# A decode kernel of attention beside a Mish layer: an early end of the Tile context, a PSUM bank of its own for w1, and w2 behind the turn

## The chip, the cores and the metric

The kernel runs on one core of a Trainium2 chip. Its time is the device time in microseconds. Three runs gave 1307.58, 1308.07 and 1309.73 us; the median, 1308.07, is the time before. The engines are called PE (TensorE), DVE (VectorE), ACT (ScalarE), POOL (GpSimd) and SP (SyncE, which here only issues transfers). PEld is the loading of weights into PE.

## The reference

One token for each of 8 batches (D = 512) goes through a layer norm, and the normed row feeds two branches whose results are added to x:

```
xn = layernorm(x)
A  = softmax(q k^T / sqrt(128)) v  @ wo      # q = xn @ wq, 32 query heads, 8 K/V heads,
                                             # 8192 cached positions, heads of 128
Bm = mish(xn @ w1 + b1) @ w2                 # F = 1792; mish(h) = h * tanh(softplus(h))
out = x + A + Bm
```

All is float32. The caches of K and V are 268 MB each, so 561 MB are read once and nearly nothing is written.

## The kernel before, in words

The work is cut into 16 packs p; each has two batches b and a pair of K/V heads. A K block or a V block of one (p, b) is 8.4 MB. Three places in SBUF take what is loaded: `kva` and `kvb`, for K, V, w1 and w2, and `kvw`, for a quarter of wq or wo. `plan` puts each load on a list in a fixed order (K(p, b), then V(p-1, b)), and `pump` issues the head of the list on SP as soon as the place it wants is free; `release` frees a place when the last product that read it is done. SP's queue is in order, so a load whose place is held also holds those behind it.

What the places see: wq, then w1 (into `kva`) and K(0,0) (into `kvb`) at the start; K(0,1) goes into `kva` behind w1; from then on K goes into `kvb` (which has some room for the next K's overlap) and V into `kva`. At the end V(15,0) goes into `kvb`, V(15,1) into `kva` in two parts, and behind V(15,0) come, in turn, w2's first part, half of wo's last quarter, w2's second part, the other half of wo, and w2's last part.

The start, pack "before" (enter(0)): `setup` clears some buffers on DVE, norms x and builds selectors; `queries` forms the queries of four heads in the PSUM bank H on PE, which DVE scales and turns and `expand`s into qT; `mish` forms xn @ w1 + b1, also in H, so its first product waits until DVE has read the queries there; DVE tells SP (a `relay`, a wait that passes a signal on) that w1 is read, and copies the result out.

In a pack: `scores` (64 products into c), `rows` (into s), `maximum` (DVE and PE), `expand` for the next pack's queries, `exponents` (ACT and DVE), `weights`, and `values` for the pack before (into o), then `gather` and `merge`. PE, DVE and ACT run these as loops over the packs 1 to 15.

The end (enter(PACKS)): the last `values`, `gather(1)`, then the products of aT with w2 (`down`), `merge(1)`, `collect(1)`, `turn` (which brings the heads' results into oW, copied out by DVE and ACT), `last_outputs` (oW with wo) and more `down`, all summed up in H; DVE copies H to acc, SP sends it out. `unread` is filler: products that nobody reads.

The class Program records each operation with its waits; `emit` then issues them, within `tc.tile_critical`; `tc.close` ends the Tile context, with two barriers of all engines, and `finish` clears the semaphores and waits for the transfer out. As all operations are issued from one helper, all have line 390 in the profile; they are told apart by their tiles (c<-kvb,qT are scores, o<-kva,pt values, h<-kvb,aT the products of w2, h<-kvw,oW those of wo, h<-acc,gsel the bias of w1).

Of the kernel before, what the change touches and what calls it, by code (L numbers as in the profile page):

```python
# [28 lines left out]
FG = F // G  # L29
# [4 lines left out]
PB = 2  # L34
# [75 lines left out]
class Program:  # L110
# [8 lines left out]
    def __init__(self, nc):  # L119
        self.nc = nc  # L120
        self.ops, self.count = [], {}
        self.know = {e: {} for e in ENGINES}
        self.seen = {}
        self.on_chip, self.psum = set(), set()
        self.pack, self.name, self.zone, self.at = None, None, "before", 0
        self.sends, self.numbers = {}, {}
        self.starts, self.sems = {}, {}

# [56 lines left out]
    def add(self, op, after=()):  # L185
# [161 lines left out]

    def finish(self, stream):

        (last,) = (c for c in self.signals if c[0] == stream)  # L350
        numbers = sorted(s.num for c, s in self.sems.items() if c != last)
        assert numbers == list(range(numbers[0], numbers[-1] + 1))
        self.nc.gpsimd.sem_clear(range(numbers[0], numbers[-1] + 1))
        self.nc.sync.wait_ge(self.sems[last], 16).then_inc(self.sems[last], -16)

    def emit(self):
        self.schedule()
        self.verify()
        nc, sems, unit = self.nc, self.sems, {}
        for c, given in sorted(self.signals.items(), key=lambda x: x[0][0] == "out"):  # L360
            sems[c] = nc.alloc_semaphore("_".join(x for x in c if x))
            unit[c] = given[0].unit

        def lower(engine, c, n):
            n *= unit[c]
            if n:
                getattr(nc, engine).wait_ge(sems[c], n).then_inc(sems[c], -n)

        def values(o):
            if o.place[1] == "loop" and o.engine in LOOPED:  # L370
                return [(c, n * unit[c]) for c, n in self.body[o.place].items()]
            top = {}
            for g in o.waits:
                c = self.channel(g)
                n = self.number[g]
                if o.engine in LOOPED and o.place[1] == "after":
                    n -= self.lowered(c, END, self.final)
                top[c] = max(n * unit[c], top.get(c, 0))
            return list(top.items())

        def issue(o, pack):
            engine = getattr(nc, o.engine)
            *first, last = values(o) or [None]
            for c, n in first:
                engine.wait_ge(sems[c], n)
            if o.method in ("settle", "relay"):
                got = engine.wait_ge(sems[last[0]], last[1])
            else:
                args, kw = (o.make(pack), {}) if o.make else (o.args, o.kw)
                got = getattr(engine, o.method)(*args, **kw)  # L390
                if last:
                    got.wait_op(sems[last[0]], last[1], "sem-ge")
            if c := self.channel(o):
                got.then_inc(sems[c], o.unit)

        for o in self.ops:
            if o.place[1] == "before" or o.engine not in LOOPED:
                issue(o, o.pack)
        for engine, parts in self.bodies():
# [19 lines left out]
            for o in self.ops:  # L419
                if o.place[1] == "after" and o.engine == engine:  # L420
                    issue(o, o.pack)


@with_exitstack
def kernel(
# [173 lines left out]
    def setup():  # L599
# [78 lines left out]
    def setup_w1(xs):  # L678
# [13 lines left out]

        pool.memset(pt, 0.0, after=[read])

# [30 lines left out]

    def expand(later):

        for b in range(PB):
            dve.vary(
# [9 lines left out]

    def scores(b, k, order, relay=False):  # L740
# [11 lines left out]
        read = prog.relay("scalar", "sync", last) if relay else None  # L752
        act.copy(sc, C[b])
        return read
# [11 lines left out]

    def maximum():
# [179 lines left out]
    def mish(w1_sb):  # L947


        hp = H[:, :FG]  # L950
        for g in range(G):
# [73 lines left out]
    for p in range(PACKS):  # L1025
        prog.enter(p)
        for b in range(PB):
            k = landed.pop(("k", p, b))
            n = PB * p + b - (p > 0)
            order = range(KR) if n % 2 == 0 else range(KR - 1, -1, -1)  # L1030
            read = scores(b, k, order, relay=(p, b) == (0, 1))
            release(("k", p, b), read)
# [10 lines left out]
            elif p > 0:  # L1043
                merge(0)
            rows(b)
            if b == 1:
                maximum()
                expand(1)
                exponents(0)
                fold()  # L1050
# [52 lines left out]
    tc.compile()  # L1103
    prog.finish("out")

# [37 lines left out]
```

## Time and profile before

| | |
|---|---|
| median of three runs | 1308.07 us |
| profiled execution | 1307.95 us |
| its span, first to last instruction | 1305.8 us |
| PE busy | 875.6 us, 67% of the span |
| DVE busy | 389.9 us, 30% |
| ACT busy | 122.2 us, 9% |
| POOL busy | 4.8 us |
| read from HBM | 561.01 MB |
| mean granted clock of PE | 0.834 |

All rows of the trace come from the one profiled execution; times in them are microseconds from the start of its span. In a stretch's row stand its bounds and length, then for PE, PEld, DVE, ACT and POOL the busy time and the number of instructions, then the granted share of PE's clock, the mean busy share of the 16 DMA engines (which can be over 1 in a short stretch) and GB/s. In the chain, each row has a start, a duration and what the time went to; "DMA" is the time from a transfer's issue to its landing. In the timeline a row has start, duration, engine, line, operation, out<-in, the shape and how many instructions were merged; in brackets the engine's idle time before it and what ended it. A float32 product of PE shows as two records.

### The profile page before, as it was taken

How to read it: one execution, taken by the hardware profiler on the slowest of the kernel's cores; microseconds unless marked ns; L12 is line 12 of the kernel's file. 1: busy time of each engine (PE TensorE's matmuls, PEld its weight loads, DVE VectorE, ACT ScalarE, POOL GpSimd, SP SyncE). 2: the span in 40 equal slices, each digit the busy share in tenths (PEclk: the TensorE clock that was granted, in tenths of full speed). 3: DMA queues.
4: the chain of work that ended last, by engine and by line, in shares of the span. 5: the costliest groups of instructions: out<-in, count | busy, mean ns of one | idle time of the engine just before them, and what ended most of it. 6: DMA issues, size and time to landing. Idle time of an engine off the chain costs nothing.

```text
span 1305.8 us, 11349 instructions
## 1 busy us (share of the span) xinstructions
PE 875.6 (67%) x4798; PEld 274.0 (21%) x4798; DVE 389.9 (30%) x596; ACT 122.2 (9%) x294; POOL 4.8 (0%) x10
## 2 busy tenths in 40 slices
PE   4886657766657765687666686665875755766568
PEld 1221112212112211122111222111221211222113
DVE  5350504305051230521405132052320515014061
ACT  0020202001020110201102020010200102001020
POOL 1000000000000000000000000000000000000000
PEclk8887788887789877898887888778887779878878
DMA  9999999999999999999999999999999999999997
GB/s 402 446 422 442 422 444 424 442 426 442 426 442 426 440 424 444 424 442 426 442 426 442 417 448 428 440 426 434 434 434 434 434 434 428 440 428 440 428 434 324
DMA packets 11409, 561.21 MB, mean 430 GB/s; under 512 B 1276, under 2 KB 1408, under 8 KB 1544
## 3 DMA queue, kind: packets, MB, share of 16 engines
q1 hardware_dynamic: 11376, 561.06, 99.5%
q8 instruction: 7, 0.11, 0.0%
q10 hardware_dynamic: 24, 0.02, 0.0%
q14 instruction: 2, 0.02, 0.0%
HBM read 561.01 MB, written 0.07 MB: 430 GB/s over the span
## 4 chain that ended last, share of the span: by engine, by line
DMA 63%; PE 34%; DVE 2%; issue 0%; POOL 0%; ACT 0%; DVEq 0%; ACTq 0%; SPq 0%
DMA kvb<-in_kT 60%; PE c L390 30%; PE h L390 2%; DMA kva<-in_kT 2%; PE o L390 1%; DMA kvb<-in_w 1%; DVE raw L390 1%; PE m L390 0%; DVE pt L390 0%; DVE wide L390 0%; DVE nm L390 0%; DVE st L390 0%; PE s L390 0%; POOL pt L390 0%; DMA sc<-in_x 0%
## 5 line engine op out<-in xcount | busy, mean ns | idle before, releaser
L390 PE MATMUL c<-kvb,qT 128*64 128x512 f32 x1984 | 497.7, 665 | 327.3 <-DMA kvb<-in_kT 325.6
L390 PEld LDWEIGHTS c<-kvb,qT 128*64 128x64 f32 x1984 | 153.3, 154 | 671.7 <-DMA kvb<-in_kT 354.5
L390 PE MATMUL o<-kva,pt 128*32 128x512 f32 x1984 | 241.5, 643 | 25.4 <-DMA kva<-in_v 24.9
L390 DVE TENSOR_REDUCE nm<-s 128x1 f32<-128x1024 f32 x16 | 19.6, 1225 | 444.6 <-PE s L390 444.6
L390 DVE STREAM_TRANSPOSE raw<-wide 128x2048 f32<-128x2048 f32 x36 | 125.4, 3483 | 15.9 <-ACT wide L390 14.0
L390 ACT COPY sc<-c 128x512 f32<-128x512 f32 x32 | 18.8, 586 | 974.7 <-PE c L390 974.7
L390 PEld LDWEIGHTS o<-kva,pt 128*32 128x32 f32 x1984 | 65.4, 117 | 192.8 <-issue 149.2
L390 ACT ACTIVATE wide<-s,nms 128x512 f32<-128x512 f32 x128 | 88.0, 688 | 129.8 <-DVE nms L390 66.3
L390 DVE TENSOR_TENSOR oT<-m,rt 128x16 f32 (+1 forms) x17 | 3.0, 175 | 230.9 <-PE m L390 230.9
L390 DVE TENSOR_SCALAR os<-o,isel 128x128 f32<-128x128 f32 x32 | 11.2, 350 | 153.9 <-PE o L390 153.9
L390 DVE TENSOR_TENSOR pt<-raw 64x256 f32<-64x256 f32 x128 | 53.5, 418 | 1.9
L390 PE MATMUL s<-sc,csel 64*128 64x512 f32 x128 | 37.1, 657 | 8.7 <-ACT sc L390 7.1
L390 DVE TENSOR_TENSOR qT<-qc,bsel 128x1024 f32<-128x1024 f32 x34 | 40.1, 1222 | 1.0
L390 DVE TENSOR_TENSOR raw<-raw 128x1024 f32<-128x1024 f32 x32 | 39.2, 1225 | 2.9
L390 DVE SCALAR_TENSOR_TENSOR os<-o,isel,os 128x128 f32<-128x128 f32 x96 | 33.7, 351 | 3.4
L390 ACT ACTIVATION_READ_ACCUMULATOR wide<-s,nms 128x1 f32 x128 | 24.7, 193 | 0.0
L390 PE MATMUL m<-hsel,os 128*128 128x8 f32 x66 | 12.7, 265 | 10.5 <-DVE lsel L390 10.5
L390 PE MATMUL m<-ident,nm 128*1 128x128 f32 x16 | 4.4, 276 | 21.6 <-DVE nm L390 21.6
L390 PE MATMUL h<-kvw,xnT 128*64 128x512 f32 x64 | 16.9, 676 | 0.0
L390 DVE TENSOR_SCALAR wide<-h 128x512 f32<-128x512 f32 x16 | 11.1, 691 | 19.2 <-PE h L390 18.8
L390 PEld LDWEIGHTS m<-hsel,os 128*128 128x128 f32 x66 | 10.1, 193 | 24.7 <-issue 12.4
L390 PE MATMUL c<-kva,qT 128*64 128x512 f32 x64 | 14.0, 594 | 0.6 <-DMA kva<-in_kT 0.6
(91 smaller groups left out, 169.4 us busy)
## 6 DMA issues: line engine op xcount, KB each, us to landing
kvw<-in_wq SPq DMA_DIRECT2D x4, 2048.0 KB, 30.1
kvw<-in_wo SPq DMA_DIRECT2D x3, 2048.0 KB, 30.7
kva<-in_v SPq DMA_DIRECT2D x1, 6144.0 KB, 24.6
kva<-in_w SPq DMA_DIRECT2D x1, 3584.0 KB, 15.9
kva<-in_v SPq DMA_DIRECT2D x1, 2048.0 KB, 29.1
kvb<-in_w SPq DMA_DIRECT2D x1, 2048.0 KB, 14.1
kvw<-in_wo SPq DMA_DIRECT2D x2, 1024.0 KB, 18.1
kvb<-in_w SPq DMA_DIRECT2D x1, 1024.0 KB, 17.9
```

Of the source, the lines that this page charges most:

```text
L390: got = getattr(engine, o.method)(*args, **kw)
```

## The change

It has five parts.

- The program is prepared first (`prepare`: schedule, verify, semaphores). Within the Tile context only the first operations are issued: of each engine those ahead of its first operation that waits (`emit_first`). These are the two transfers of ACT, SP's first three, six clearings on DVE and one on POOL. Then the context is closed, with its barriers, and the rest is issued outside it. At the end SP passes the wait of its transfer out on to POOL (semaphore `end`), which clears the semaphores while SP waits for the landing.
- xn @ w1 + b1 goes into the bank O[1] instead of H; DVE clears that bank at the start. POOL, and not DVE, relays to SP and to DVE that the products are done.
- V(0,0) is loaded in two halves, the upper one first: it is issued when half of the products with K(0,1) are done (that block is read from its upper end).
- In pack 0, DVE expands the next queries as soon as `scores` of a batch are done: for batch 0 in its own turn, for batch 1 between the two parts of `maximum`.
- At the end, `unread(2)` stands behind the last `values`; w2's first part (4 of 7 rows, 32 products, 64 records) is multiplied behind `turn` instead of around `merge(1)`.

```diff
@@ Program.add
-            if know.get(other.who, -1) < other.n:
+            if know.get(other.who, -1) < other.n or op.method == "relay":
...
+    def emit_first(self):
+        waiting = set()
         for o in self.ops:
-            if o.place[1] == "before" or o.engine not in LOOPED:
+            if o.waits:
+                waiting.add(o.engine)
+            if o.engine not in waiting and o.place[1] == "before":
+                self.issue(o, o.pack)
+                self.done.add(o)
...
+    def finish(self, stream):
...
+        end = self.nc.alloc_semaphore("end")
+        (c, n), *_ = self.values(self.signals[last][0])
+        self.nc.sync.wait_ge(self.sems[c], n).then_inc(end, 1)
+        self.nc.gpsimd.wait_ge(end, 1).then_inc(end, -1)
+        self.nc.gpsimd.sem_clear(range(numbers[0], numbers[-1] + 1))
+        self.nc.sync.wait_ge(self.sems[last], 16).then_inc(self.sems[last], -16)
...
+    def load_early():
+        what, _, load = queue.pop(0)
+        landed[what] = load()
...
-            if p > 0:
+            if p == 1 and b == 0:
+                plan_v(0, 0, "a", "v1", (1 / 2, 1))
+                plan_v(0, 0, "a", part=(0, 1 / 2))
+            elif p > 0:
                 plan_v(p - 1, b, "a")
...
         dve.memset(H, 0.0)
+        dve.memset(O[1], 0.0)
...
         for r in order:
+            if first and r == order[KR // 2]:
+                load_early()
...
         pe.transpose(M[:1, 0:P], nm, ident)
+        if first:
+            expand(1, [1])
...
-        hp = H[:, :FG]
+        hp = O[1][:, :FG]
...
-        read = prog.relay("vector", "sync", last)
+        read = prog.relay("gpsimd", "sync", last)
+        done = prog.relay("gpsimd", "vector", last)
...
-        dve.tensor_copy(h, hp)
+        dve.tensor_copy(h, hp, after=[done])
...
     values(1, landed["v", p, 1], ROUNDS * 3 // 4)
+    unread(2)
     gather(1)
-    w2_sb, wo_sb = landed["w2"], landed["wo", PAIRS - 1]
-    down(0, 2, w2_sb)
     merge(1)
     collect(1)
-    down(2, W2_PARTS[0][1], w2_sb)
     turn(last=True)
+    w2_sb, wo_sb = landed["w2"], landed["wo", PAIRS - 1]
+    down(*W2_PARTS[0], w2_sb)
     last_outputs(0, OR // 2, wo_sb)
...
+    prog.prepare()
     with tc.tile_critical(no_gpsimd_drain=True):
-        prog.emit()
+        prog.emit_first()
     tc.close()
     tc.compile()
+    prog.emit()
     prog.finish("out")
```

More of the change, by code (lines that the diff above doesn't have):

```diff
@@ L126, in __init__ @@
         self.sends, self.numbers = {}, {}
[L127 removed]
+        self.starts, self.sems, self.unit = {}, {}, {}
     def __getattr__(self, engine):
@@ L346, in bodies, with prepare @@
             yield e, [(by_pack[min(by_pack)], at) for at, by_pack in sorted(parts.items())]
[L348 to L356, printed above, removed]
+    def prepare(self):
@@ L357, in emit @@
         self.schedule()
         self.verify()
-        nc, sems, unit = self.nc, self.sems, {}
         for c, given in sorted(self.signals.items(), key=lambda x: x[0][0] == "out"):
[L361 to L394, printed above, removed]
@@ L396, in emit, with lower, values @@
-        for o in self.ops:
-            if o.place[1] == "before" or o.engine not in LOOPED:
+            self.sems[c] = self.nc.alloc_semaphore("_".join(x for x in c if x))
+            self.unit[c] = given[0].unit
+        self.done = set()
+    def lower(self, engine, c, n):
+        n *= self.unit[c]
+        if n:
+            getattr(self.nc, engine).wait_ge(self.sems[c], n).then_inc(self.sems[c], -n)
+    def values(self, o):
+        if o.place[1] == "loop" and o.engine in LOOPED:
+            return [(c, n * self.unit[c]) for c, n in self.body[o.place].items()]
+        top = {}
+        for g in o.waits:
+            c = self.channel(g)
+            n = self.number[g]
+            if o.engine in LOOPED and o.place[1] == "after":
+                n -= self.lowered(c, END, self.final)
+            top[c] = max(n * self.unit[c], top.get(c, 0))
+        return list(top.items())
@@ new lines, in issue @@
+    def issue(self, o, pack):
+        engine = getattr(self.nc, o.engine)
+        *first, last = self.values(o) or [None]
+        for c, n in first:
+            engine.wait_ge(self.sems[c], n)
+        if o.method in ("settle", "relay"):
+            got = engine.wait_ge(self.sems[last[0]], last[1])
+        else:
+            args, kw = (o.make(pack), {}) if o.make else (o.args, o.kw)
+            got = getattr(engine, o.method)(*args, **kw)
+            if last:
+                got.wait_op(self.sems[last[0]], last[1], "sem-ge")
+        if c := self.channel(o):
+            got.then_inc(self.sems[c], o.unit)
@@ L398, in emit @@
+    def emit_first(self):
+        waiting = set()
+        for o in self.ops:
+            if o.waits:
[3 more added lines that the diff above has]
+                self.done.add(o)
+    def emit(self):
+        nc, issue, lower = self.nc, self.issue, self.lower
+        for o in self.ops:
+            if o not in self.done and (o.place[1] == "before" or o.engine not in LOOPED):
                 issue(o, o.pack)
@@ L421, in emit @@
                     issue(o, o.pack)
+    def finish(self, stream):
+        (last,) = (c for c in self.signals if c[0] == stream)
+        numbers = sorted(s.num for c, s in self.sems.items() if c != last)
+        assert numbers == list(range(numbers[0], numbers[-1] + 1))
+        end = self.nc.alloc_semaphore("end")
[4 more added lines that the diff above has]
+        self.nc.sync.wait_ge(self.sems[last], 16).then_inc(self.sems[last], -16)
 @with_exitstack
@@ L691, in setup_w1 @@
             )
-        pool.memset(pt, 0.0, after=[read])
+        pool.memset(pt, 0.0, after=[read], to="vector")
     def queries(w):
@@ L724, in queries, with expand @@
         return read
-    def expand(later):
-        for b in range(PB):
+    def expand(later, batches=range(PB)):
+        for b in batches:
             dve.vary(
@@ L738, in expand, with scores @@
             )
-    def scores(b, k, order, relay=False):
+    def scores(b, k, order, first=False):
         t = qT[:, b].rearrange("p r u h -> p r (u h)")
         for r in order:
+            if first and r == order[KR // 2]:
+                load_early()
             for c in range(2):
@@ L751, in scores @@
                 )
-        read = prog.relay("scalar", "sync", last) if relay else None
+        read = prog.relay("scalar", "sync", last) if first else None
         act.copy(sc, C[b])
@@ L1030 @@
             order = range(KR) if n % 2 == 0 else range(KR - 1, -1, -1)
-            read = scores(b, k, order, relay=(p, b) == (0, 1))
+            read = scores(b, k, order, first=(p, b) == (0, 1))
             release(("k", p, b), read)
@@ L1045 @@
             rows(b)
+            if (p, b) == (0, 0):
+                expand(1, [0])
             if b == 1:
-                maximum()
-                expand(1)
+                maximum(first=p == 0)
+                if p > 0:
+                    expand(1)
                 exponents(0)
```

2 lines of the change are left out of this document (1 added, 1 removed).

## The prediction

> **What bounds the kernel now.** I read the page first: the DMA row of the slices and the share of the one big queue.
>
> ```profile
> DMA  9999999999999999999999999999999999999997
> q1 hardware_dynamic: 11376, 561.06, 99.5%
> ```
>
> The reader is to see that the DMA engines work in every slice but the last. PE's products hold buffers, but while K's buffer is held, V's transfer fills the same engines. Whether anything is to be gained inside is read from the stretches.
>
> ```profile
> core 0: us, PE busy (x) PEld busy (x) DVE busy (x) ACT busy (x) POOL busy (x), PEclk, DMA share, GB/s
> 2.20:38.00 35.80, 17.54 (x102) 5.14 (x102) 19.12 (x45) 2.99 (x4) 3.98 (x3) 0.84 0.99 420
> 38.00:1294.00 1256.00, 849.33 (x4570) 262.38 (x4574) 369.01 (x545) 118.47 (x288) 0.00 (x0) 0.84 1.00 433
> ...
> 1300.20:1305.80 5.60, 3.20 (x64) 2.23 (x56) 0.29 (x1) 0.00 (x0) 0.00 (x0) 0.74 0.04 12
> ```
>
> From 2.2 to 1294 us the DMA share is 0.99 to 1.00, at 433 GB/s for 1256 us: a saturated stream. The change moves the same bytes, so nothing done under this stream shortens it, unless it starts earlier. What is left is the last 5.6 us, in which almost nothing is transferred (12 GB/s): there PE finishes and the result goes out. So the change is judged there, and at the head only for whether it starves the stream.
>
> **The change, part by part: the head.** The first rows are of the timeline, the next of the chain, the last is the landing time of the first K transfer.
>
> ```profile
> 1.44 0.48 DVE L390 MEMSET h<- 128x512 f32 x1
> ...
> 1.86 0.50 SPq L390 DMA_DIRECT2D kvb<-in_kT  x1
> ...
> 2.79 0.67 DVE L390 TENSOR_REDUCE st<-sc 8x1 f32<-8x512 f32 x1 [0.58 <-DMA sc<-in_x]
> ...
> 23.84 1.68 PE L390 MATMUL h<-acc,gsel 4*8 4x448 f32 x8 [6.21 <-DVEq L387]
> ...
> 33.99 0.33 SPq L390 DMA_DIRECT2D kva<-in_kT  x1
> ```
>
> ```profile
> 11.79 5.86 PE h L390 x16
> ...
> 23.84 10.07 PE h L390 x72
> ```
>
> ```profile
> DMA to landing us min/median/max: 36.0/36.0/36.0
> ```
>
> What closing the Tile context costs is shown at the end of the program, where it stands now:
>
> ```profile
> L1103 POOLq EVENT_SEMAPHORE  x4: 17/17/17, 1304.7 to 1305.5; - x4
> ...
> L1103 SPq DRAIN  x3: 7/7/7, 1304.6 to 1304.9; - x3
> ```
>
> ```profile
> 1303.79 0.35 SPq L390 DMA_DIRECT2D out<-acc  x1
> ```
>
> ```profile
> out<-acc SPq DMA_DIRECT2D x1, 64.0 KB, 1.5
> ```
>
> SP's last issue ends at 1303.79 + 0.35 = 1304.14 and the second barrier is through at 1305.5: the closing takes some 1.4 us. In the change it begins behind SP's third issue (1.86 + 0.50 = 2.36) and behind VectorE's memsets, so ends near 3.8, and the first reduction moves from 2.79 to about 3.9: every step of the setup 1.1 us later (between 0, if it fits beside the wait for x, and 1.5). SP's three transfers are issued ahead of it, so the stream starts as before. VectorE's added memset of a PSUM bank (0.48, as the one of h) ends near 2.7 and lies under x's landing and that closing.
>
> What covers this 1.1 us is the next deadline of the stream. K(0,1) is issued at 33.99, when w1's products have been read; the first K lands at 1.86 + 36.0 = 37.9, so 3.9 us were in hand. In the change w1's 72 products (products are counted here as the profile's records, two of each) no longer wait 6.21 us for VectorE to read the queries' bank; they follow the queries directly (11.79 + 5.86 + 1.1 = 18.8) and take at most 10.07, so SP is told by 28.8, with GpSimd's two relays a few tenths later: 5 us earlier than now, closing included. That is worth 0 if the stream has not a hole there, and at most what the first 38 us lack against the steady rate: 35.8 x (1 - 420/433) = 1.07 us. I take 0: the share there is 0.99, and the transfers of the start are of smaller pieces. Both ends go into the range. Without this cover, the closing would cost its 1.1 us.
>
> In pack 0 the expansion of the next queries (2 VectorE instructions) is moved ahead of the maxima, and V(0,0) comes in two halves, the upper one issued when half of K(0,1) is used. On SP the early half stands behind K(1,0)'s issue and ahead of the lower half; what waits behind it is only the lower half, which waits longer anyway. Same bytes, one more issue of 0.33 beside an idle SP, under a saturated stream: 0. If the cover went, the price would be VectorE's expansion, about 1 us, once.
>
> **The tail.** First the chain, then the timeline around it.
>
> ```profile
> 1277.40 14.13 DMA kvb<-in_w
> ...
> 1291.57 1.06 PE h L390 x32
> 1292.63 0.32 PE m L390 x2
> 1292.95 1.82 PE h L390 x32
> 1294.78 1.91 PE m L390 x8
> ...
> 1297.37 6.07 PE h L390 x112
> ...
> 1303.47 0.29 DVE acc L390
> ```
>
> ```profile
> 1277.52 1.93 PE L390 MATMUL c<-sc,ones 128*32 128x512 f32 x16
> ...
> 1289.30 1.12 DVE L390 SCALAR_TENSOR_TENSOR os<-o,isel,os 128x128 f32<-128x128 f32 x3
> ...
> 1292.99 0.17 DVE L390 TENSOR_TENSOR oT<-m,rt 128x16 f32<-128x16 f32 x1 [2.57 <-PE m L390]
> ...
> 1302.44 0.95 PE L390 MATMUL h<-kvb,aT 128*8 128x128 f32 x16
> ```
>
> The five last transfers are issued together (1277.4 to 1279.5) and land one after the other; first the two of wo, then the three of w2, from issue to landing:
>
> ```profile
> L390 SPq DMA_DIRECT2D kvw<-in_wo x2: 426/430/435, 1277.8 to 1279.0; - x2
> ...
> DMA to landing us min/median/max: 16.2/18.1/20.0
> ```
>
> ```profile
> L390 SPq DMA_DIRECT2D kvb<-in_w x3: 328/328/426, 1277.4 to 1279.5; - x3
> ...
> DMA to landing us min/median/max: 14.1/17.9/20.7
> ```
>
> So w2's first part is there at 1277.4 + 14.1 = 1291.5, wo's first half at 1277.8 + 16.2 = 1294.0, w2's second part near 1296.5 (median of three, issued at about 1278.6), wo's second half at 1279.0 + 20.0 = 1299.0, w2's last part at 1279.5 + 20.7 = 1300.2. PE's last product ends near 1303.4, so PE is 3.2 us behind the last landing. Why it is behind is read from the granted clock (the column before the DMA share):
>
> ```profile
> 71.10:74.30 3.20, 1.13 (x4) 0.30 (x4) 1.22 (x1) 0.59 (x1) 0.00 (x0) 1.00 0.85 369
> 74.40:81.10 6.70, 4.35 (x12) 1.61 (x14) 4.89 (x7) 3.12 (x8) 0.00 (x0) 0.50 1.00 430
> ...
> 1207.60:1210.90 3.30, 1.72 (x16) 0.55 (x20) 0.00 (x0) 0.00 (x0) 0.00 (x0) 1.00 0.87 377
> 1211.00:1214.00 3.00, 3.00 (x36) 0.91 (x32) 0.00 (x0) 0.00 (x0) 0.00 (x0) 1.00 1.01 437
> ```
>
> ```profile
> 1288.84:1291.57 2.73, 0.00 (x1) 0.00 (x0) 1.40 (x4) 0.00 (x0) 0.00 (x0) 1.00 0.96 393
> 1291.57:1292.88 1.31, 1.31 (x34) 1.07 (x34) 0.00 (x0) 0.00 (x0) 0.00 (x0) 1.00 1.03 432
> 1292.90:1296.60 3.70, 3.70 (x41) 2.82 (x40) 0.17 (x1) 0.00 (x0) 0.00 (x0) 0.50 1.01 420
> ```
>
> PE stands still for 2.73 us, waiting for w2's first part; at 1292.9 the clock is halved, and the same 32 products take 1.82 us where they took 1.06 just before. All that follows runs at half speed, the last 112 in 6.07.
>
> In the change 8 filler products (unread, 16 records) stand where PE stood still, 1.93 us by the row of the same filler: they run from 1288.84 to about 1290.7, while VectorE gathers until 1289.30 + 1.12 = 1290.42. Merge and turn follow. Step by step, at full clock: merge and VectorE's product 0.6 (now 1292.63 to 1292.99 + 0.17), to 1291.3; turn half of 1.91, 1.0, to 1292.3; w2's first part, now landed, 64 products at 1.06 per 32, 2.1, to 1294.4 (the copies to oW, 1296.7 to 1297.3 now, lie beside them, and cost that 0.6 where they don't). wo's first half is there: 1.06, to 1295.5. Then PE waits for landings: w2's second part 1296.5 + 1.06 = 1297.6, wo's second half 1299.0 + 1.06 = 1300.1, w2's last part 1300.2 + half of 1.06 and about 0.1 of latency = 1300.8. VectorE's last copy starts there and not at 1303.47: 2.6 us gained. Moving w2's first 64 products behind the turn adds nothing: in this order they are paid once, before landings that end later. A wait goes, and what is late next are the landings themselves.
>
> **The tail's end.** After the last copy starts, now 0.32 to SP's issue (1303.47 to 1303.79), 1.5 to the landing, then what is left of the closing: the span ends at 1305.8, 2.33 behind the copy. In the change SP only waits for the landing, and GpSimd clears the semaphores beside it: 0.32 + 1.5 + 0.1 = 1.9. Gain 0.4 (0 if the end takes as long as now).
>
> **The sum.** The profiled execution took 1307.95 us, span 1305.8; 2.15 lie around it, which I leave as they are. 1307.95 - 2.6 - 0.4 = 1304.95. The profiled execution stands 0.12 under the median of 1308.07, so against the median 1305.1, 0.23% less. A measurement of this kernel tells about 0.2%, 2.6 us, from no change: the forecast stands just beyond that line (1305.45).
>
> **The rivals.**
>
> A, the forecast: PE keeps its full clock to the end and waits for landings. 1305.1, own range 1304.7 to 1305.6.
>
> B: the clock is halved in the new waits. Between 1295.5 and 1299.0 PE is busy for 1.06 us of 3.5. The rows speak for it: 1.13 busy of 3.20 is followed by half clock, 1.72 of 3.30 is not. Against it: only a stretch lying nearly across both waits is that empty, so it depends on where the gate looks. Price: wo's second half 1299.04 + 1.82 = 1300.9, then the last 16 at 0.95 and latency (1302.44 to 1303.47, 1.03) = 1301.9, 1.1 later than A: 1306.2; 1305.6 where the drop comes halfway. The Trainium skill, in "TensorE: Matmul & The Clock Gate", Part 1 (the HAM clock gate), has the clock fall after at least one idle window of about 3.4 us, the windows running free. Taken literally, waits of 1.0 and 1.4 us would never halve it and A would hold; the trace differs, as 2.73 us of standing still (1288.84 to 1291.57) and 1.13 busy of 3.20 both brought half clock.
>
> C: the filler doesn't hold the clock, PE runs at half from 1292.9 as now. Turn done at 1292.3, 64 products at half clock, 2 x 1.82 = 3.6, to 1296.0, the last 112 in 6.07 without a wait, 1302.1, copy at 1302.2: 1.3 gained, with the closing 1.7: 1306.4. For it: merge and turn are thin work, and in 1292.90 to 1296.60 PE was busy throughout without getting its clock back. Against it: the filler makes this stretch busier than any row that fell.
>
> D, the other side: the closing, now in mid-program, waits for the transfers in flight. Then the setup begins at 37.9 and not at 2.8, K(0,1) is issued 31 us after that (33.99 - 2.79) less the 6.21 and, with PE cold as now, at about 63, and the stream stands still for some 25 us: 1330. It decides as soon as SP's drain holds until more than 5.6 us behind the landing at 37.9 are lost (3.0 gained and 2.6 the line). Against it: SP's drains at the end last 7 ns each, at 1304.6 to 1304.9, while the out transfer is in flight until 1303.79 + 1.5 = 1305.3.
>
> E: the earlier K(0,1) closes a hole in the stream: up to 1.07 more, all landings of the tail with it: 1304.0.
>
> **How the numbers follow.** A 0.52, B 0.25, C 0.10, E 0.09, D 0.04. Faster by over 0.2% are E and five sixths of A: 0.53. Slower is D with little else beside it: 0.04. Within 0.2%: B, C and the rest of A: 0.43. The range runs from 1304.0 (E) to 1306.5 (B and C). It leaves out D and what lies beyond C and E.
>
> **What would show it.** Right: PE's MATMUL h<-acc, gsel replaced by products into o right behind the queries, with no wait on VectorE; SP's K(0,1) issue at 24 to 29 us; the steady stretch at 433 GB/s; c<-sc, ones filler at 1288.9; h products of the tail at 1.06 per 32, each group behind a landing of w2 or wo; the last copy 0.6 behind w2's last landing; no barrier rows behind the out transfer. Wrong: granted clock 0.50 behind 1296 (B) or 1293 (C); no transfer running in the head near 35 us (D); the span's end moved less than the last copy.

## The result, and the profile after

The changed kernel takes 1304.14 us (median of 12 executions, 1303.98 to 1304.89). The kernel before, executed in between on the same chips, took 1307.67 (median of 12, 1305.05 to 1310.51). The ratio is 0.9975, interval 0.9966 to 0.9984: faster by a quarter of a per cent, which is just beyond what this kernel's measurement can tell. The profiled execution took 1304.17, with a span of 1302.8.

The spreads deserve as much attention as the medians: before, 5.5 us lie between the fastest and the slowest execution; after, 0.9 us. The fastest execution of the kernel before, 1305.05, is only 0.9 above the median of after.

The page of the changed kernel, the slices' DMA row and the big queue:

```profile
DMA  9999999999999999999999999999999999999998
q1 hardware_dynamic: 11520, 561.06, 99.7%
```

Its stretches, in the columns known from before (bounds, length, busy time of PE, PEld, DVE, ACT and POOL, granted clock, DMA share, GB/s):

```profile
2.20:38.00 35.80, 14.19 (x102) 4.85 (x104) 26.80 (x56) 3.34 (x4) 4.42 (x5) 0.89 1.00 426
38.00:1294.00 1256.00, 856.16 (x4602) 272.10 (x4602) 361.87 (x539) 118.74 (x290) 0.00 (x0) 0.83 1.00 433
...
1300.20:1302.80 2.60, 0.62 (x16) 0.34 (x16) 0.29 (x1) 0.00 (x0) 0.00 (x0) 1.00 0.09 25
```

The stream is as it was, 433 GB/s. What has become shorter is the stretch behind the last landing: 2.6 us where there were 5.6. The head, from the timeline (start, duration, engine, line, operation, out<-in; all operations are now issued from line 383):

```profile
3.77 0.67 DVE L383 TENSOR_REDUCE st<-sc 8x1 f32<-8x512 f32 x1 [1.01 <-PEq L1138]
...
18.17 0.93 PE L383 MATMUL o<-acc,gsel 4*8 4x448 f32 x8
19.04 6.20 PE L383 MATMUL o<-kva,aT 128*8 128x448 f32 x64
...
25.35 0.33 SPq L383 DMA_DIRECT2D kva<-in_kT  x1
```

The setup begins at 3.77 instead of 2.79, because it now stands behind the closing (L1138). The products of w1 follow the queries without a wait, and K(0,1) is issued at 25.35 instead of 33.99. The closing and the end, from the lines' starts:

```profile
L1138 SPq DRAIN  x3: 7/7/7, 3.0 to 3.3; - x3
...
L1138 POOLq EVENT_SEMAPHORE  x4: 17/17/17, 3.1 to 3.6; - x4
...
L438 SPq EVENT_SEMAPHORE  x1: 17/17/17, 1302.8 to 1302.8; - x1
```

The barriers are over at 3.6, with the first transfers in flight, and the last instruction is SP's wait for the landing. The tail's timeline:

```profile
1288.69 1.90 PE L383 MATMUL c<-sc,ones 128*32 128x512 f32 x16
1290.52 0.39 PE L383 MATMUL m<-hsel,os 128*128 128x8 f32 x2
1291.17 1.10 PE L383 MATMUL m<-oT,wide 128*128 128x64 f32 x8 [0.27 <-DVE oT L383]
1292.21 1.93 PE L383 MATMUL h<-kvb,aT 128*8 128x128 f32 x64
1294.05 1.06 PE L383 MATMUL h<-kvw,oW 128*8 128x128 f32 x32
1296.52 1.06 PE L383 MATMUL h<-kvb,aT 128*8 128x128 f32 x32 [1.41 <-DMA kvb<-in_w]
1299.01 1.06 PE L383 MATMUL h<-kvw,oW 128*8 128x128 f32 x32 [1.42 <-DMA kvw<-in_wo]
1300.23 0.62 PE L383 MATMUL h<-kvb,aT 128*8 128x128 f32 x16 [0.16 <-DMA kvb<-in_w]
...
1300.92 0.29 DVE L383 COPY acc<-h 128x128 f32<-128x128 f32 x1 [8.04 <-PE h L383]
1301.24 0.35 SPq L383 DMA_DIRECT2D out<-acc  x1
```

The filler stands where PE stood still, every 32 products take 1.06, and the last three groups wait in brackets for landings, not for PE.

Between the two profiled executions the time went in three places: the last copy starts at 1300.92 instead of 1303.47 (2.55); from there to the span's end it takes 1302.8 - 1300.92 = 1.88 instead of 2.33 (0.45); and around the span lie 1304.17 - 1302.8 = 1.37 instead of 2.15 (0.78). Together 3.78. But a profiled execution is one of twelve, and those of the kernel before spread over 5.5 us. What has to be explained is also why after's do not.

### The profile page after: what moved, and what is told of

Read it like the earlier page. It is cut to its first block, busy times and chain, and to the rows that moved or that the text cites. A ratio compares the mean times of both kernels' runs of the same rounds, so it can differ in the third digit from the quotient of the medians.

```text
span 1302.8 us, 11368 instructions
## 1 busy us (share of the span) xinstructions
PE 874.2 (67%) x4814; PEld 279.6 (21%) x4814; DVE 389.9 (30%) x597; ACT 122.1 (9%) x294; POOL 4.8 (0%) x10
## 4 chain that ended last, share of the span: by engine, by line
DMA 66%; PE 32%; DVE 1%; issue 0%; SPq 0%; ACT 0%; DVEq 0%
DMA kvb<-in_kT 65%; PE c L383 30%; DMA kvb<-in_w 2%; PE o L383 1%; DVE raw L383 0%; DVE pt L383 0%; SPq L383 0%; DVE os L383 0%; DVE nm L383 0%; PE s L383 0%; PE m L383 0%; PE h L383 0%; ACT sc L383 0%; DVE acc L383 0%; DVE nr L383 0%
## 5 line engine op out<-in xcount | busy, mean ns | idle before, releaser
L383 PEld LDWEIGHTS c<-kvb,qT 128*64 128x64 f32 x1984 | 161.1, 154 | 669.1 <-issue 470.7
L383 PE MATMUL o<-kva,pt 128*32 128x512 f32 x1984 | 244.7, 650 | 24.7 <-DMA kva<-in_v 24.1
```

## The experiments

The theory is the prediction's: PE's clock in the tail carries the gain, the head carries none. The rivals: the head carries it, through a transfer that came too late in some executions; and, on a smaller scale, that filler, moved w2 or closing alone carry it. The table gives all runs. "Over 1306" counts executions above that time; "around" is the median of what lies between span and time (spans are known to 0.1).

| kernel | executions | median us | range | over 1306 | median span | around |
|---|---|---|---|---|---|---|
| before, all jobs | 109 | 1307.46 | 1305.01 to 1311.86 | 66 | | 2.1 |
| after | 12 | 1304.14 | 1303.98 to 1304.89 | 0 | 1302.8 | 1.38 |
| no filler | 8 | 1304.05 | 1303.92 to 1304.16 | 0 | 1302.7 | 1.40 |
| closing late | 12 | 1305.15 | 1305.02 to 1305.26 | 0 | 1303.2 | 1.94 |
| new tail alone | 12 | 1305.38 | 1305.0 to 1309.49 | 5 | 1303.3 | 2.08 |
| filler alone | 12 | 1305.34 | 1305.14 to 1308.49 | 5 | 1303.2 | 2.10 |
| old head | 11 | 1305.61 | 1304.45 to 1307.79 | 4 | 1304.3 | 1.57 |
| K(0,1) late | 10 | 1309.27 | 1308.94 to 1311.08 | 10 | 1307.8 | 1.47 |
| all engines end last | 11 | 1304.53 | 1304.37 to 1305.52 | 0 | 1302.9 | 1.62 |
| new head alone | 11 | 1305.10 | 1304.98 to 1307.66 | 2 | 1303.2 | 1.93 |
| V(0,0) whole | 11 | 1304.08 | 1303.92 to 1307.19 | 2 | 1302.7 | 1.35 |
| K(0,1) at 33 | 10 | 1304.27 | 1304.08 to 1304.87 | 0 | 1302.75 | 1.45 |
| K(0,1) at 33, again | 10 | 1304.22 | 1304.08 to 1304.80 | 0 | 1302.8 | 1.47 |
| waits filled | 11 | 1303.91 | 1303.77 to 1304.21 | 0 | 1302.5 | 1.37 |

### The filler taken out

```diff
 values(1, landed["v", p, 1], ROUNDS * 3 // 4)
-unread(2)
 gather(1)
```

> The changed kernel without the filler behind the last values; w2 stays behind the turn. Theory (the filler holds PE's clock): PE stands still from 1288.8 to 1290.5, does thin work (merge, turn) until 1292.3, and in those executions where the gate looks at that stretch the clock is halved near 1292 to 1293; the 64 products of w2 then take 3.6 us and the last 112 some 6, the last copy starts near 1302.2 instead of 1300.9, time 1305.4; in the others 1304.1. Rival (the move of w2 behind the turn is what gains, the filler does nothing): clock 1.00, 1304.1 in all executions.

It is no slower: 1304.05. Its stretches and the tail's timeline:

```profile
1288.73:1290.37 1.64, 0.01 (x2) 0.01 (x1) 1.40 (x4) 0.00 (x0) 0.00 (x0) 1.00 0.99 410
1290.40:1292.70 2.30, 2.03 (x34) 1.88 (x38) 0.59 (x3) 0.41 (x2) 0.00 (x0) 1.00 0.97 399
1292.80:1296.10 3.30, 3.30 (x71) 2.62 (x67) 0.00 (x0) 0.00 (x0) 0.00 (x0) 0.50 1.02 425
1296.20:1303.00 6.80, 2.97 (x92) 1.92 (x84) 0.29 (x1) 0.00 (x0) 0.00 (x0) 1.00 0.40 158
```

```profile
1292.06 2.97 PE L383 MATMUL h<-kvb,aT 128*8 128x128 f32 x64
...
1298.91 1.06 PE L383 MATMUL h<-kvw,oW 128*8 128x128 f32 x32 [1.42 <-DMA kvw<-in_wo]
...
1300.80 0.29 DVE L383 COPY acc<-h 128x128 f32<-128x128 f32 x1 [8.08 <-PE h L383]
```

The clock is halved, and the 64 products take 2.97 instead of 1.93. It costs nothing: with w2's products behind the turn PE stands still for only 1.64 us instead of 2.73, is then busy throughout, and has its clock back after 3.3 us of that; the landing at about 1298.9 takes up what was lost. In the kernel before, with neither filler nor the new order, half clock went on to the last products, through 3.70 us of unbroken work, a pause of 0.70 and then 5.73 us more:

```profile
1297.37:1303.10 5.73, 5.73 (x109) 4.45 (x112) 0.00 (x0) 0.00 (x0) 0.00 (x0) 0.50 0.22 90
```

So the clock's return after 3.30 us is what one execution shows, and not a rule; that nothing is lost is shown by all 8 times. The Trainium skill, in "TensorE: Matmul & The Clock Gate", Part 1 (the HAM clock gate), gives the clock back after a busy window of about 3.4 us, the windows running free. The 3.30 us here are near that, and the 5.73 us do not contradict it: where a window may begin at any time, up to twice its length can pass before a whole one is busy, some 6.8 us, an estimate from the page's figure.

### The closing at the end again

```diff
     with tc.tile_critical(no_gpsimd_drain=True):
         prog.emit_first()
+        prog.emit()
     tc.close()
     tc.compile()
-    prog.emit()
```

With it goes SP's early word to POOL, on which POOL clears the semaphores beside the landing.

> The changed kernel with the Tile context closed at the end, as before. Theory: the last copy starts at 1300.9 as in the changed kernel, the span ends 2.3 behind it (1303.2), and the time around the span is 2.15 again: 1305.4, that is 1.2 more than the changed kernel, 0.4 of it in the span and 0.8 around it. Rival (the time around the span was a chance difference): 1304.6, only the 0.4.

1305.15, 1.0 more than after, in every execution (1305.02 to 1305.26). The end of its chain and the stretch from the last copy:

```profile
1300.88 0.29 DVE acc L383
```

```profile
1300.88:1303.20 2.32, 0.00 (x0) 0.00 (x0) 0.29 (x1) 0.00 (x0) 0.00 (x0) 1.00 0.10 28
```

The copy starts as in after (1300.92). So the closing costs 2.32 - 1.88 = 0.44 within the span and 1.94 - 1.38 = 0.56 around it. The second part lies where no row of a profile shows it.

### All engines made to wait for the end

```diff
+over = {e: self.nc.alloc_semaphore(f"over_{e}") for e in LOOPED}
+for sem in over.values():
+    self.nc.sync.wait_ge(self.sems[last], 16).then_inc(sem, 1)
 self.nc.sync.wait_ge(self.sems[last], 16).then_inc(self.sems[last], -16)
+for e, sem in over.items():
+    getattr(self.nc, e).wait_ge(sem, 1).then_inc(sem, -1)
```

> The changed kernel with PE, VectorE and ScalarE made to wait, as their last instruction, until SP has seen the result land. Theory (the time around the span is what the last engines have to do behind their last instruction; engines that end early do it under the transfer out): the span grows by some 0.2, the time around it from 1.4 to 2.1; 1305.0. Rival (the 0.8 around the span belongs to the two barriers of the closing alone): 1304.3.

Here PE, DVE and ACT finish behind the landing, as they did behind the closing's barriers. The time around the span is 1.62, neither the 2.1 of the theory nor after's 1.38. At most 0.24 of the 0.56 come back, and even that is not shown to be the engines' ends: old head, which ends just as after does, stands at 1.57, K(0,1) late at 1.47. What sets the time around the span stays open. The profiled execution showed something else, in stretches and timeline:

```profile
1295.15:1299.10 3.95, 1.12 (x36) 0.83 (x40) 0.00 (x0) 0.00 (x0) 0.00 (x0) 1.00 0.85 348
1299.15:1302.50 3.35, 2.63 (x48) 1.78 (x42) 0.29 (x1) 0.00 (x0) 0.00 (x0) 0.50 0.04 15
```

```profile
1299.05 1.89 PE L383 MATMUL h<-kvw,oW 128*8 128x128 f32 x32 [1.41 <-DMA kvw<-in_wo]
...
1301.83 0.29 DVE L383 COPY acc<-h 128x128 f32<-128x128 f32 x1 [8.88 <-PE h L383]
```

This is rival B: 1.12 us busy in 3.95, then half clock, and the last copy at 1301.83 instead of 1300.92, 0.9 late (priced at 1.1). PE's work ahead of it is after's, so it can befall after too: the three executions of after at 1304.69 to 1304.89 fit that size, but have no profile. Here 4 of 11 executions, 1305.14 to 1305.52, stand 0.6 to 1.0 above the other seven. The prediction gave one row on each side of the limit, 1.13 us busy of 3.20 and 1.72 of 3.30; the profile of before has a third, 1.39 of 3.40 (from 1245.1 on), which half clock also followed, so the limit, as far as such rows place it, lies nearer to a half than to a third. Taken literally, the rule of the Trainium skill ("TensorE: Matmul & The Clock Gate", Part 1), an idle window of about 3.4 us, would not have halved the clock between waits of 1.41 and 1.42; being thinly busy was enough here.

### The new tail alone, and the filler alone

Both are made on the kernel before. The first:

```diff
+unread(2)
 gather(1)
-w2_sb, wo_sb = landed["w2"], landed["wo", PAIRS - 1]
-down(0, 2, w2_sb)
 merge(1)
 collect(1)
-down(2, W2_PARTS[0][1], w2_sb)
 turn(last=True)
+w2_sb, wo_sb = landed["w2"], landed["wo", PAIRS - 1]
+down(*W2_PARTS[0], w2_sb)
```

The second has only the added `unread(2)`, in front of the old order.

> The kernel before with the new tail alone (filler, and w2 behind the turn). Theory: head and pack 0 are worth nothing under the saturated stream, so this is as the changed kernel closed late: last copy at 1300.9, 1305.4. Rival (the earlier K(0,1) closes a hole in the stream): all landings of the tail up to 1.07 later than in the changed kernel, so 1306.4.

> The kernel before with the filler alone; w2's first part stays around the merge. Theory: clock 1.00 through the tail; PE waits for w2's first part at 1291.5, does everything 2.8 us later than behind the turn but still ahead of the landings at 1299.0 and 1300.2, so the last copy starts at 1300.9 all the same: 1305.4, equal to the whole tail. Rival (the move is needed): PE ends as before, 1307.7.

Medians 1305.38 and 1305.34: the filler alone does what the whole tail does. But 5 of 12 executions of each are over 1306, up to 1309.49, and both profiles fell among them. Filler alone, the timeline of its tail:

```profile
1291.92 1.90 PE L390 MATMUL c<-sc,ones 128*32 128x512 f32 x16
...
1293.72 1.06 PE L390 MATMUL h<-kvb,aT 128*8 128x128 f32 x32
...
1301.15 1.06 PE L390 MATMUL h<-kvw,oW 128*8 128x128 f32 x32 [1.40 <-DMA kvw<-in_wo]
1302.37 0.62 PE L390 MATMUL h<-kvb,aT 128*8 128x128 f32 x16 [0.15 <-DMA kvb<-in_w]
...
1303.06 0.29 DVE L390 COPY acc<-h 128x128 f32<-128x128 f32 x1 [5.34 <-PE h L390]
```

The clock is full throughout (1.06 per 32), yet the filler starts 3.2 us later than in after, and the last copy 2.14, since PE waits for landings which are late themselves. Where they became late is in the chains of the two (start, duration, what). First filler alone, then new tail alone:

```profile
34.41 24.60 DMA kva<-in_kT
```

```profile
24.43 10.42 PE h L390 x72
34.92 24.79 DMA kva<-in_kT
...
1304.46 0.67 PE h L390 x16
1305.15 0.29 DVE acc L390
```

K(0,1) is in the chain, and lands at 59.01 and 59.71. In the kernel before it was issued at 33.99 and landed at 57.10. The two issues are 0.4 and 0.9 later, the landings 1.9 and 2.6. Around the issue less is transferred; first the kernel before, then new tail alone (filler alone: 321 GB/s):

```profile
34.00:40.00 6.00, 2.06 (x6) 0.77 (x8) 5.14 (x10) 0.58 (x1) 0.00 (x0) 0.73 0.84 354
34.00:40.00 6.00, 2.79 (x18) 0.76 (x8) 4.23 (x9) 0.58 (x1) 0.00 (x0) 0.84 0.86 319
```

The products of w1 are partly at half clock in all three, and take 10.07 in the kernel before, 10.12 and 10.42 here, where after's take 0.93 + 6.20 = 7.1. So most of the delay lies ahead of them: in filler alone they begin 0.39 later (x landed 0.28 later, the products of the queries took 0.10 more), in new tail alone 0.59 later (the products of the queries took 6.56, not 5.86). So the head has a hole after all, in some executions. That is rival E, which had only the first 38 us in view.

### K(0,1) made late on purpose

```diff
-read = prog.relay("gpsimd", "sync", last)
 done = prog.relay("gpsimd", "vector", last)
...
-return read
+return prog.relay("vector", "sync", done)
```

In the changed kernel, DVE now tells SP at the end of `mish`, behind all its work.

> The changed kernel with one wait more: SP is told that w1 is read only when VectorE is through with the Mish, so K(0,1) is issued at 39.3 and not at 25.3, 1.4 us behind the landing of the first K. Theory (each microsecond of a hole in the stream comes out at the end): K(0,1) lands 4 to 5 us later, near 61.5, as does everything behind it; 1308.5. Rival (pack 0 has slack that takes it up): 1304.1.

K(0,1)'s transfer and the end of the chain:

```profile
L383 SPq DMA_DIRECT2D kva<-in_kT x1: 328/328/328, 38.7 to 38.7; - x1
...
DMA to landing us min/median/max: 21.8/21.8/21.8
```

```profile
1305.89 0.29 DVE acc L383
```

And the stretch around its issue, in which DMA share and GB/s are the last two columns:

```profile
34.00:40.00 6.00, 2.26 (x6) 0.77 (x8) 4.75 (x7) 0.00 (x0) 0.00 (x0) 0.50 0.41 142
```

There is the hole: a share of 0.41 over 6 us. (A row counts a packet in the stretch in which it begins.) In after the same six microseconds moved 371 GB/s. The last copy comes 4.97 later than in after (1305.89 against 1300.92), and all 10 executions are at 1308.9 or above. The late issue alone costs 5 us, where 4.4 were expected. The landing of K(0,1) is 3.3 later than in after (60.53 against 57.23); the next K lands 20.6 behind it instead of 19.35, 1.25 more. Why that second gap opens, and where the last 0.4 goes, stays open. How the hole comes about can be read from the packets in the trace: 14 of the 16 DMA engines end their last packet of the first K by 36.12, the last of them at 37.25, ahead of the landing told at 37.69; the first packet of K(0,1) begins at 39.70, 0.96 behind its issue, and the first ones take 2.6 to 3.4 us each, where 2.42 is usual.

### K(0,1) at 33, twice

```diff
-read = prog.relay("gpsimd", "sync", last)
 done = prog.relay("gpsimd", "vector", last)
...
+read = prog.relay("vector", "sync", done)
 dve.reciprocal(z, t1)
```

The second has the same relay behind the reciprocal, to reach a shorter lead.

> The changed kernel with K(0,1) told by VectorE in the middle of the Mish, just ahead of its reciprocal: issue near 32.8, 5.0 ahead of the first K's landing at 37.8. Theory (a lead of some 4 us or more is enough): no hole, K(0,1) lands at 57.1, 1304.1. Rival (any issue later than the changed kernel's costs): more than 1304.5.

> The same, told just behind the reciprocal: issue near 35.8, 2.0 ahead of the landing. Theory: the engines run dry one after the other before the new packets reach them, K(0,1) lands 1 to 3 us later than 57.1, median 1306, no execution at 1304.1. Rival (my prediction: no hole before 37.9): 1304.1.

1304.27 and 1304.22, spreads as in after. The second edit missed its aim, as its timeline shows:

```profile
32.89 2.95 DVE L383 RECIPROCAL wide<-wide 128x448 f32<-128x448 f32 x1
32.95 0.33 SPq L383 DMA_DIRECT2D kva<-in_kT  x1
```

SP's issue came 0.06 behind the reciprocal's start, not behind its end. So the two are one measurement made twice, at a lead of 4.5 to 4.7. With it the profiles give the price of a late issue (K(0,1) lands some 19.3 behind the first K when no hole is between; "lead" is the first landing less the issue):

| kernel | K(0,1) issued | first K landed | lead | K(0,1) landed |
|---|---|---|---|---|
| after | 25.35 | 37.87 | 12.5 | 57.23 |
| K(0,1) at 33 | 32.93 | 37.67 | 4.7 | 57.02 |
| K(0,1) at 33, again | 32.95 | 37.49 | 4.5 | 56.84 |
| old head | 33.76 | 37.83 | 4.1 | 57.03 |
| before | 33.99 | 37.90 | 3.9 | 57.10 |
| filler alone | 34.41 | 37.94 | 3.5 | 59.01 |
| new tail alone | 34.92 | 37.96 | 3.0 | 59.71 |
| K(0,1) late | 38.74 | 37.69 | -1.0 | 60.53 |

A lead of 3.9 or more cost nothing. At 3.5 K(0,1) landed 59.01 - 37.94 = 21.1 behind the first K, so 1.8 late; at 3.0 it was 2.5 late, and at -1.0 3.5. The profiled execution of before stood at most 0.4 us on the good side of that edge. The packets show how near: in it the engines end their last packets of the first K between 35.5 and 36.8, and those of K(0,1) begin from 35.58 on, just in time; in filler alone they end between 35.3 and 36.9, but the new ones begin from 35.57 to 38.0 and take 2.7 to 3.75 us at first.

### The old head with the rest new

w1 back in H with DVE's relay, V(0,0) whole, `expand` in its old place; closing early and tail new.

```diff
-hp = O[1][:, :FG]
+hp = H[:, :FG]
...
-read = prog.relay("gpsimd", "sync", last)
-done = prog.relay("gpsimd", "vector", last)
+read = prog.relay("vector", "sync", last)
...
-if p == 1 and b == 0:
-    plan_v(0, 0, "a", "v1", (1 / 2, 1))
-    plan_v(0, 0, "a", part=(0, 1 / 2))
-elif p > 0:
+if p > 0:
     plan_v(p - 1, b, "a")
...
```

> The changed kernel with its head as before (w1's products in H, told by VectorE, V(0,0) whole, the queries expanded behind the maxima); early closing and new tail stay. Theory (a load must be issued some 3.5 us or more ahead of the landing before it, or the stream has a hole): the closing puts the setup 1.0 later, K(0,1) is issued at 35 to 36, 2 to 3 us ahead of the landing at 37.9; K(0,1) then lands 1 to 4 us later than 57.1, the executions spread from 1304.1 to 1309, median 1306. Rival (my prediction: no hole before 37.9): K(0,1) lands at 57.1, all executions at 1304.1.

1305.61 (1304.45 to 1307.79), 1.5 above after in the median, and 4 of 11 over 1306. Its profile caught no hole (lead 4.1), but rival B once more: 1.10 us busy of 3.93, then half clock, the last copy at 1301.73, 0.81 late. The time around the span, 1.57, is 0.19 above after's. So the 1.5 is not the price of the head. What speaks for holes are the 4 over 1306, since rival B and those 0.19 together would end near 1305.2; what the five at 1305.47 to 1305.87 have lost stays open.

### The new head alone

After with the closing late and the tail of before: pack "before" and pack 0 are all that is new.

```diff
-unread(2)
 gather(1)
+w2_sb, wo_sb = landed["w2"], landed["wo", PAIRS - 1]
+down(0, 2, w2_sb)
 merge(1)
 collect(1)
+down(2, W2_PARTS[0][1], w2_sb)
 turn(last=True)
-w2_sb, wo_sb = landed["w2"], landed["wo", PAIRS - 1]
-down(*W2_PARTS[0], w2_sb)
```

> The kernel before with the new head and pack 0 alone; context closed at the end, tail as before. Theory: no holes in the stream, so no execution above 1308; the tail still waits for w2's first part and loses its clock in part of the executions: two groups, at 1305.1 and at 1307.5, median 1307.4, near the kernel before. Rival (the head is worth nothing): the same spread as before, 1305.0 to 1309.7.

1305.10, the same as with both (1305.15, the closing late), and not the 1307.4 that was expected: the clock is lost more rarely than the theory had it. Two of 11 stand apart, at 1307.59 and 1307.66. The profile is of one that doesn't:

```profile
1289.39:1291.37 1.98, 0.01 (x2) 0.01 (x1) 1.40 (x4) 0.00 (x0) 0.00 (x0) 1.00 0.98 397
1291.40:1294.70 3.30, 3.30 (x74) 2.77 (x74) 0.17 (x1) 0.00 (x0) 0.00 (x0) 1.00 1.01 420
```

In this execution the old tail kept its clock: PE stood still for 1.98 us, not for 2.73 as in the profile of before. Old order and no filler thus lose the clock in some executions only. That the two at 1307.6 are these is argued from their distance, 2.5 us, near the 2.55 that the last copy gained; no profile shows them.

### V(0,0) whole

```diff
-if p == 1 and b == 0:
-    plan_v(0, 0, "a", "v1", (1 / 2, 1))
-    plan_v(0, 0, "a", part=(0, 1 / 2))
-elif p > 0:
+if p > 0:
...
-if first and r == order[KR // 2]:
-    load_early()
```

> The changed kernel with V(0,0) loaded whole, as before; all else of the head stays (w1's products in their own bank, the queries expanded early). Theory (only K(0,1)'s early issue closes the hole): V(0,0) is issued at 71.2, 5.3 ahead of the landing at 76.5, no hole, 1304.1 with the same narrow spread. Rival (V's early half closes a second hole): some executions 1 to 2 us longer.

1304.08 in the median, as after, but 2 of 11 at 1306.31 and 1307.19, where after has none of 12. The halves may guard a second place: in the profile of the new tail alone V(0,0) was issued at 76.57, 2.6 ahead of the landing before it, and K(1,1) then landed 20.6 behind V(0,0) rather than 19.4, while V(0,0) itself was on time (19.4 behind K(1,0)). This is argued; no profile shows it in the kernel with V(0,0) whole.

### The waits filled

Rival B's cause taken away: eight records of filler in each of the two waits of the tail, and the last part of w2 in halves.

```diff
-W2_PARTS = ((0, 4), (4, 6), (6, 7))
+W2_PARTS = ((0, 4), (4, 6), (6, 6.5), (6.5, 7))
...
 last_outputs(0, OR // 2, wo_sb)
+unread(1)
 down(*W2_PARTS[1], w2_sb)
+unread(1)
 last_outputs(OR // 2, OR, wo_sb)
 down(*W2_PARTS[2], w2_sb)
+down(*W2_PARTS[3], w2_sb)
```

> The changed kernel with four more filler products in each of PE's two waits of the tail, and w2's last part cut in two halves of 256 KB. Theory: PE never is empty enough for its clock to be halved, so the executions at 1304.7 to 1304.9 go; behind the last landing stand 8 records instead of 16, 0.2 less: 1303.9 in all. Rival (smaller pieces land later, the last landing sets the end): 1304.1 or more.

1303.91 (1303.77 to 1304.21), the fastest of all; ratio to before 0.998, interval 0.9971 to 0.9989. Its stretches and timeline:

```profile
1295.15:1299.10 3.95, 3.64 (x88) 2.11 (x80) 0.00 (x0) 0.00 (x0) 0.00 (x0) 1.00 0.89 355
```

```profile
1299.76 0.79 PE L383 MATMUL h<-kvb,aT 128*8 128x128 f32 x16
...
1300.62 0.29 DVE L383 COPY acc<-h 128x128 f32<-128x128 f32 x1 [6.78 <-PE h L383]
```

PE is busy for 3.64 us of the stretch that held 1.12 in the profile of all engines ending last, and no execution is slower than 1304.21. That rival B is gone by it is likely, but not shown: no filler (8 executions) and closing late (12) have no late ones either, with their waits unfilled. The last copy starts 0.3 earlier, as behind the last landing only half as many products are left.

## Why the prediction was right, and where it was not

The time was right: 1305.1 forecast, 1304.14 measured, inside the range, and faster as the likelier case had it. The steps are less even.

**Right.** The stream: 433 GB/s in the steady stretch on both sides. The setup: 1.1 us later expected, 0.98 measured. SP told by 28.8: issue at 25.35. The tail, step by step: turn done at 1292.3 (1292.27), w2's first part to 1294.4 (1294.1), wo's first half to 1295.5 (1295.1), last copy at 1300.8 (1300.92). The closing within the span: 0.4, measured 0.45. Rival D is excluded: SP's drains last 7 ns each at 3.0 to 3.3, while the first K is in flight until 37.87.

**The term that was mis-sized: the 2.15 around the span, "which I leave as they are".** They became 1.37. The closing put back at the end restores 0.56 of the 0.78. Together the closing is worth 1.0, not 0.4, and that, not the tail, is most of what put the time 1.0 below the forecast. Whether the engines' ends have a part in it is not shown; what sets it stays open.

**The step that failed in the head: "I take 0", with 3.9 us in hand.** That holds for the profiled execution and for no more. The products of w1 end earlier or later by an execution, as x lands, the queries' products run and PE has its clock, and where the lead of K(0,1) falls to 3.5 or less the stream has a hole of 1.8 us or more. In the two kernels with old head, old closing and a filled tail, 10 of 24 executions are over 1306; with the new head, the old closing and the new tail, none of 12. Rival E named the mechanism. Its bound of 1.07, though, came from the share of the first 38 us in an execution without a hole, and the hole lies behind 34 us and costs 1.8 to 2.5 at the next landing in the two executions with the old head, 3.5 there and 5 at the end with K(0,1) late.

**The step that was right for the wrong comparison: the tail's 2.6.** It was measured between the profiles (2.55), and filler alone on the kernel before shows full clock. But not all executions of the kernel before lose that clock. Of its 109, 43 are below 1306, taken here as those with neither loss; 54 lie from 1306 to 1308.7; 12 are above that. An estimate from the runs: if holes come in 10 of 24 and the clock is lost independently in a share s, then (1 - 0.42)(1 - s) = 43/109 gives s = 0.32, and both together 0.42 x 0.32 = 13%; 12 of 109, 11%, are in the highest group. The estimate is rough: new head alone, where only the clock can be lost, has 2 of 11, 18%; and new tail alone reaches 1308.96 and 1309.49 by holes only, so the highest group need not be both losses. So the runs speak for two separate losses of 2 to 2.5 us, each in some part of the executions, and the change removes both. The forecast found one of them, which happened to be the one in the profiled execution, and the median of before stands where either alone puts it. That the sum came out is in part luck.

**The step that failed in the reasons: "Moving w2's first 64 products behind the turn adds nothing", and the filler as what holds the clock.** Either is enough. Without the filler the new order reaches 1304.05; without the new order the filler reaches the same median as both on the kernel before. With the new head, the old tail alone reaches the same median too (1305.10, the closing late), so that either edit is needed for a few executions only. Rival C (a filler that doesn't hold the clock) was seen in no profile.

**Rival B** is real, and as frequent as its chance of 0.25 had it: seen in two profiles of the changed tail (all engines ending last, old head), 0.9 and 0.8 us; 4 of 11 executions of the first by their times, perhaps three of after's 12, 0.55 to 0.75 above its median; none of 11 with the waits filled.

**Pack 0's edits at nothing**: `expand`'s move showed no cost in any run and was not tried alone; V's halves do nothing to the median, and may guard 2 of 11 executions.

## What to carry to other kernels

Where a saturated stream bounds a kernel, ask for each load how far its issue is ahead of the landing before it, and ask it over the spread of executions: a margin that just suffices in one profile is a loss in others. A median of a kernel whose executions stand in groups is a statement on how often each loss occurs, so take the losses away one at a time and count the executions per group. Barriers at this program's end cost 1.0 us, more than half of it outside the span; at its start they lay beside transfers already in flight and cost nothing that the runs show.

## What the runs showed of the hardware

- With transfers of 8.4 MB at 433 GB/s, K(0,1) issued 3.9 us or more ahead of the landing before it followed without a gap; at 3.5 its landing was 1.8 late, at 3.0 2.5. The DMA engines end their last packets 0.4 to 2.7 us before that landing is told (35.3 to 37.25 against 37.7 to 37.9), and the first packet of the next transfer begins 1.0 to 1.2 us behind its issue where an engine is free. The edge was measured for this transfer only: V(0,0), issued 2.6 ahead in new tail alone, landed on time, and the transfer behind it 1.2 late.
- PE's clock was halved after 1.12 us of work in 3.95, after 1.39 in 3.40, and after 2.73 us of standing still; it was kept after 1.72 us of work in 3.30, and after 1.98 us of standing still in one execution. It came back after 3.30 us of unbroken work in one execution, and had not after 5.73 in another.
- A DVE relay placed behind a reciprocal of 2.95 us passed 0.06 us after that reciprocal began: the wait was passed on while the engine still computed. So did the one behind the last copy in K(0,1) late (copy at 38.68, issue at 38.74).
- The time around the span depends on how the program ends: 2.1 us in before, 1.94 with the new head and tail but the closing late, 1.38 with the closing early, 1.62 with all engines held to the end. Old head, with after's end, has 1.57, so that it depends on more than the end.
